# Layer-norm sums in float32r, weight conversions moved earlier, and finer matmul groups in an attention + FFN + gMLP kernel

## The chip, the cores and the metric

One core of a Trainium2 chip runs one program. The metric is the device time in microseconds of one execution, as a median over runs; a profile of one further execution shows where its time goes. TensorE is called PE (its weight loads PEld), VectorE DVE, ScalarE ACT, GpSimd POOL; all DMAs are issued by SyncE (SP).

## What is computed

Four batches of 448 tokens, model width 768, all in float32:

```python
scores = cap * tanh(q @ k.T / 8 / cap)              # 12 heads of 64
x = softmax(scores) @ v                             # heads side by side: (4, 448, 768)
xn = (x - mean(x)) / sqrt(var(x) + 1e-6) * g_ln     # layer norm over the 768 features
x = x + relu(xn @ w_ch1) @ w_ch2                    # FFN, inner width 3072
u, v = split(relu(x @ w_in))                        # gMLP, 512 + 512
v_n = (v - mean(v)) / sqrt(var(v) + 1e-6)
out = (u * (w_spatial @ v_n + b_spatial)) @ w_out
```

## The kernel before

Features lie on partitions: a tile holds 128 features x 448 tokens. A product with float32 accuracy is made of three float32r matmuls: each operand is split into a high part (a copy rounded to float32r) and a low part (value minus high part), and `hi*hi`, `hi*lo`, `lo*hi` are added in PSUM (`mm3`). Attention, and the column sums of the layer norm, use plain float32 matmuls. The program has a lead (attention of batches 0 and 1, with their layer norms), then for each pair of batches the FFN in six groups of 4 hidden blocks (`h_units`, then `y_units`) and the gMLP (`gmlp`: `v_mm`, `u_units`, `sp_units`, `o_units`). Attention of batches 2 and 3 is spread along the first pair's FFN by `drive`.

A weight is loaded as 64-bit halves, converted to float32 on the chip, stored in a DRAM tile `kept_...` for the second pair, and split into its parts (`weight`). The conversion of one block is an ACTIVATE (times `REBASE`), a shift (TENSOR_SCALAR) and two SCALAR_TENSOR_TENSORs on DVE, all into a `wr` buffer; the split is one copy and one subtraction. There are two `w` (raw) and two `wr` buffers. `make` prepares a block ahead of its use, into `rs` buffers; before the change it does so for two blocks of `w1`.

The layer norm of batch b: `x_done` adds the twelve heads' tiles into `acc`; `ln_mean` sums `acc` over partitions on PE with a matrix of ones, then subtracts the mean, multiplies by `g_ln`, splits into parts, squares and adds the squares; `ln_scale` sums the squares on PE, with 4 x 112 tokens as the stationary operand and two columns of ones moving, forms the standard deviation and sends it through DRAM to all partitions, where DVE multiplies the residual `x` by it.

The order of instructions on each engine is made by `Program.plan`, a list scheduler with fixed costs, due times counted in PE's work, and buffer pools: 4 PSUM tiles `bank`, 2 double ones `two`. On the chip each engine then runs its own list in order, so an instruction that waits holds back all those behind it. The trace shows nearly all instructions at one line, L455, the recorder's call (L458 after the change), so they are told apart by tile names.

Of the kernel before, what the change touches and what calls it, by code (L numbers as in the profile page):

```python
# [48 lines left out]

REBASE = 2.0 ** -112  # L50

EARLY = 2
# [410 lines left out]
def attn_ffn_gmlp_kernel(  # L463
# [49 lines left out]
    ones32 = const.tile([128, 2], F32, name="ones32")  # L513
    capt = const.tile([128, 1], F32, name="capt")
# [51 lines left out]
    def weight(kind, j, home=None):  # L566
        if (kind, j) in made:
            return made.pop((kind, j))
        n = width[kind]
        if kind == "ws":  # L570
            t = hs.get()
            SP.dma_start(out=t, in_=source[kind][j])
        elif (kind, j) in kept:
            t = wr.get()[:, 0:n]
            SP.dma_start(out=t, in_=kept[kind, j])
        else:
            raw = w6.get()[:, 0:n]
            SP.dma_start(out=raw.rearrange("p n t -> p (n t)"), in_=source[kind][j].bitcast(I32))
            t = wr.get()[:, 0:n]
            ti = t.bitcast(I32)  # L580
# [9 lines left out]
            SP.dma_start(out=d, in_=t)  # L590
        if home:
# [4 lines left out]
        cp(hi, t, (A, V))  # L596
# [171 lines left out]

    def ln_mean(b):
# [5 lines left out]
        mean, sq = hs.get(), hs.get()  # L775
        A.activation(out=mean, in_=ps, func=ACTF.Copy, scale=1.0 / DM)
# [15 lines left out]
    def ln_scale(b):  # L792
        sq = ln.pop(b).rearrange("p (n c) -> p c n", c=NCT)
        ps = banks.get()
        with prog.group():
            for c in range(NCT):
                T.matmul(out=ps[0:CT, 2 * c:2 * c + 2], lhsT=sq[:, c], rhs=ones32, start=True, stop=True)
        var, rstd = (t[0:CT] for t in tok_t[b % 2])
        V.tensor_scalar(out=var, in0=ps[0:CT, 0:2 * NCT].rearrange("p (c t) -> p c t", t=2)[:, :, 0],
                        scalar1=1.0 / DM, scalar2=1e-6, op0=ALU.mult, op1=ALU.add)  # L800
# [45 lines left out]
    def v_mm(cs):  # L846

        two = [twos.get(), twos.get()]
        os = [banks.get() for _ in range(4)] + [t[:, j] for t in two for j in range(2)]
        os = os[:len(cs)]  # L850
        for k in range(KD):
            hi, lo = weight("wv", k)
            yh, yl = (t.rearrange("p a n -> p (a n)") for t in ysp[k])
            with prog.group():
                for c, o in zip(cs, os):
                    d = slice(c * 128, (c + 1) * 128)
                    for m, (l, r) in enumerate(((yh[:, d], hi), (yh[:, d], lo), (yl[:, d], hi))):
                        T.matmul(out=o, lhsT=l, rhs=r, start=(k == 0 and m == 0), stop=(k == KD - 1 and m == 2))
# [72 lines left out]
    def o_units(b, dt, ws):  # L931

        pss = [banks.get()[:, 0:S] for _ in ws]
        n = len(gs[b])
        with prog.group():
            for k, g in enumerate(gs[b]):
# [8 lines left out]
    def gmlp(bs, nxt):  # L945
# [16 lines left out]
        if nxt:  # L962
            ln_mean(first)
        vn.clear()
        for dts in ([0, 1, 2], *([dt] for dt in range(3, KD))):
            w = [weight("wo", dt) for dt in dts]
            for b in bs:
# [3 lines left out]
                else:  # L971
                    o_units(b, dts[0], w)
        gs.clear()
        if second:
            ln_mean(second)

    def h_units(bs, g, n):
# [3 lines left out]
        for m in steps:  # L981
            w = [weight("w1", j0 + j) for j in range(m)]
            j0 += m
            for b in bs:
                for j in range(m):
                    h_unit(b, w[j])
                    yield 3 * KD

    def y_units(bs, g, last):
# [3 lines left out]
        for b in bs:  # L993
            if b in ln:
                ln_scale(b)
# [42 lines left out]
    def main():  # L1038
# [6 lines left out]
        P.memset(ones32, 1.0)  # L1045
        P.memset(mhalf, -0.5)
# [3 lines left out]
        lead = attend(0, 2 * H, 1.0) + [(H + 2.25, ln_mean, (0,)), (2 * H + 2.25, ln_mean, (1,))]  # L1050
        lead += [(1.0 + j * H / EARLY, make, ("w1", j)) for j in range(EARLY)]
        drive([], lead)
        for p in range(NP):
# [3 lines left out]
                h_units(bs, g, 3 if g == 0 else 2), y_units(bs, g, g == NG - 1))))  # L1057
            n = 2 * H if p + 1 < NP else 0
            drive(units, attend(2 * H * (p + 1), n, 2 * NG * (FG * 3 * KD + KD * 3 * FG) / max(n, 1)))
# [64 lines left out]
```

## Time and profile before

| | |
|---|---|
| median of 3 runs | 1110.94 us (1109.65 to 1113.84) |
| the profiled execution | 1113.14 us, span of its instructions 1111.4 us |
| busy: PE, DVE, ACT | 1094.4, 704.7, 415.6 us |
| mean granted PE clock | 0.995 |
| chain that ended last | PE 92%, DMA 4%, ACT 1%, DVE 1% |
| DMA | 133.88 MB, mean 120 GB/s |

The span runs from the first to the last instruction. Busy time is that in which an engine has an instruction under way; matmuls overlap, so PE's busy time counts their union. The chain is followed back from the last instruction to whatever released each step.

### The profile page before, as it was taken

Reading aid. Unit: us, or ns where it says so; the run is one execution under the profiler, and the core shown is the slowest. Engines: PE = TensorE matmul, PEld = TensorE weight load, DVE = VectorE, ACT = ScalarE, POOL = GpSimd, SP = SyncE. Lnnn points to the kernel's source line nnn. Section 1 sums busy time; section 2 is a strip of 40 time slices with the busy share of each in tenths; the row PEclk is TensorE's granted clock in tenths of the full one; section 3 lists DMA queues with packets and bytes.
Section 4 is the critical chain, followed back from the end, with each engine's and each line's share of the span. In section 5 each row is a group of like instructions: output and inputs, shape, how many; then the busy total and the mean of one; then the engine's idle time right before and its main releaser. Section 6 shows DMA issues by size and latency. Waiting matters only on the chain.

```text
span 1111.4 us, 14151 instructions
## 1 busy us (share of the span) xinstructions
PE 1094.4 (98%) x5380; PEld 899.6 (81%) x5380; DVE 704.7 (63%) x1183; ACT 415.6 (37%) x615; POOL 11.1 (1%) x17
## 2 busy tenths in 40 slices
PE   8989899999999999999999999999999999999998
PEld 2323597987888878978788899999999999998988
DVE  4768789676595776958989964533343433383861
ACT  7978743545334443354444440111111111120412
POOL 0000000000000000000001000000000000000100
PEclk9989999999999999999999999999999999999999
DMA  6545354555654564554475442212121212122303
GB/s 177 126 103 147 121 154 164 173 163 171 171 174 136 158 210 139 165 162 135 152 233 189 157 142 65 67 39 76 38 76 39 67 38 76 45 62 85 102 10 109
DMA packets 80128, 133.88 MB, mean 120 GB/s; under 512 B 35598, under 2 KB 47804, under 8 KB 80060
## 3 DMA queue, kind: packets, MB, share of 16 engines
q1 hardware_dynamic: 80060, 132.98, 40.0%
q8 instruction: 42, 0.69, 0.3%
q14 instruction: 26, 0.21, 0.1%
HBM read 100.91 MB, written 32.03 MB: 120 GB/s over the span
## 4 chain that ended last, share of the span: by engine, by line
PE 92%; DMA 4%; ACT 1%; SPq 1%; DVE 1%; issue 0%; DVEq 0%
PE bank L455 86%; PE two L455 6%; DMA inv<-rc 1%; DMA rc<-sum 1%; DMA hs<-inv 1%; SPq L455 1%; ACT es L455 1%; DMA qk<-in_qk_dram 1%; DMA w<-in_w_dram 1%; ACT hs L455 1%; DMA vt<-in_v_dram 0%; DVE acc L455 0%; DVE x L455 0%; DVE es L455 0%; ACT wr L455 0%
## 5 line engine op out<-in xcount | busy, mean ns | idle before, releaser
L455 PE MATMUL bank<-rs,wh 128*128 128x448 f32 x2232 | 451.5, 362 | 0.0
L455 PEld LDWEIGHTS bank<-rs,wh 128*128 128x128 f32 x2232 | 417.8, 187 | 33.6 <-ACT wr L455 2.8
L455 PE MATMUL bank<-rb,wh 128*128 128x448 f32 x1728 | 350.7, 363 | 0.0
L455 PEld LDWEIGHTS bank<-rb,wh 128*128 128x128 f32 x1728 | 324.8, 188 | 25.1 <-DVE hs L455 3.3
L455 DVE TENSOR_TENSOR x<-bank,x 128x448 f32<-128x448 f32 x144 | 89.5, 623 | 97.5 <-PE bank L455 96.5
L455 ACT ACTIVATE wh<-wr 128x512 fp32r<-128x512 f32 (+1 forms) x89 | 63.2, 710 | 207.4 <-PE bank L455 170.9
L455 ACT ACTIVATE rb<-bank 128x448 fp32r<-128x448 f32 x96 | 52.2, 544 | 222.4 <-PE bank L455 222.3
L455 DVE SCALAR_TENSOR_TENSOR rb<-bank,rb 128x448 fp32r<-128x448 f32 x96 | 59.8, 624 | 112.3 <-ACT rb L455 111.9
L455 DVE TENSOR_TENSOR wh<-wr,wh 128x512 fp32r<-128x512 f32 (+1 forms) x150 | 117.4, 782 | 10.7 <-ACT wh L455 6.0
L455 DVE SCALAR_TENSOR_TENSOR wr<-w,wr 128x512 int32<-128x512 int32 (+1 forms) x152 | 119.2, 785 | 2.2
L455 ACT ACTIVATE wr<-w 128x512 f32<-128x512 f32 (+1 forms) x76 | 57.6, 758 | 84.1 <-DVE wh L455 35.6
L455 ACT ACTIVATE es<-two,qsc 128x896 f32<-128x896 f32 x72 | 70.9, 1009 | 24.7 <-PE two L455 24.4
L455 PE MATMUL two<-qk 64*128 64x448 f32 x288 | 69.6, 584 | 4.2 <-DMA qk<-in_qk_dram 4.2
L455 ACT ACTIVATE es<-es,capt 128x896 f32<-128x896 f32 x72 | 72.2, 1043 | 0.0
L455 DVE CAST wh<-wr 128x512 fp32r<-128x512 f32 (+1 forms) x61 | 28.8, 472 | 66.0 <-PE bank L455 48.6
L455 PE MATMUL bank<-es,vt 128*64 128x448 f32 x288 | 63.8, 557 | 0.5 <-DMA vt<-in_v_dram 0.5
L455 PEld LDWEIGHTS two<-qk 64*128 64x128 f32 x288 | 25.0, 191 | 42.6 <-issue 22.3
L455 DVE TENSOR_TENSOR es<-es,es 128x896 f32<-128x896 f32 x48 | 52.0, 1083 | 3.5 <-ACT es L455 3.2
L455 PEld LDWEIGHTS bank<-es,vt 128*64 128x64 f32 x288 | 18.1, 137 | 41.1 <-issue 30.0
L455 ACT ACTIVATE hs<-bank 128x448 f32<-128x448 f32 x49 | 26.5, 541 | 64.2 <-PE bank L455 63.6
L455 DVE TENSOR_SCALAR wr<-wr 128x512 int32<-128x512 int32 (+1 forms) x76 | 35.8, 471 | 22.8 <-ACT wr L455 22.6
L455 PE MATMUL bank<-wh,rs 128*128 128x512 f32 x144 | 35.6, 395 | 0.0
(79 smaller groups left out, 620.0 us busy)
## 6 DMA issues: line engine op xcount, KB each, us to landing
w<-in_w_dram SPq DMA_DIRECT2D x24, 768.0 KB, 5.3
w<-in_w_dram SPq DMA_DIRECT2D x36, 512.0 KB, 4.1
qk<-in_qk_dram SPq DMA_DIRECT2D x48, 224.0 KB, 3.4
kept_w<-wr SPq DMA_DIRECT2D x24, 384.0 KB, 4.9
kept_w<-wr SPq DMA_DIRECT2D x36, 256.0 KB, 4.2
wr<-kept_w SPq DMA_DIRECT2D x24, 384.0 KB, 3.9
wr<-kept_w SPq DMA_DIRECT2D x36, 256.0 KB, 2.7
out_dram<-hs SPq DMA_DIRECT2D x24, 224.0 KB, 2.1
```

What stands on the lines that cost most here:

```text
L455: fn(*(put(a) for a in args), **{k: put(a) for k, a in kw.items()})
```

## The change

Five things are changed. (1) Both column sums of a layer norm go through `feature_sum`: the summed tile is split into parts on DVE or ACT, and two float32r matmuls with a 128 x 128 matrix of ones sum them. The sum of squares now stands as a row over tokens, so `ln_scale` sends it through DRAM once more to get it as 112 x 4. (2) Centering is a function of its own (`ln_center`), and sums and centering are recorded at other points. (3) Four `w1` blocks instead of two are prepared during the first batch's heads, two of them into `wh` buffers, and the first FFN group takes all four blocks in one step; the conversion's first instruction may run on DVE as well as on ACT. (4) The conversions of the 16 gMLP weight blocks are recorded along the first FFN, from 0.3 to 0.75 of its work; the gMLP then loads the converted blocks. (5) `v_mm` and `o_units` are recorded in smaller groups and take their PSUM tiles in another order.

```diff
+AFTER = 0.3, 0.75, 0
-EARLY = 2
+EARLY = 4
...
+    onesr = const.tile([128, 128], F32R, name="onesr")
...
     def make(kind, j):
         with prog.early():
-            made[kind, j] = weight(kind, j, [rs.get().rearrange("p a n -> p (a n)") for _ in range(2)])
+            made[kind, j] = weight(kind, j, [rs.get().rearrange("p a n -> p (a n)") for _ in range(2)]
+                                   if j < 2 else [t[:, i] for t in (wh.get(),) for i in range(2)])
+    def ahead(kind, j):
+        with prog.early():
+            value(kind, j)
...
-            A.activation(out=t, in_=hi.bitcast(F32), func=ACTF.Copy, scale=REBASE)
+            with prog.either():
+                for e in (A, V) if home is None else (V, A):
+                    if e is A:
+                        A.activation(out=t, in_=hi.bitcast(F32), func=ACTF.Copy, scale=REBASE)
+                    else:
+                        V.tensor_scalar(out=t, in0=hi.bitcast(F32), scalar1=REBASE, scalar2=None, op0=ALU.mult)
...
+    def feature_sum(ps, x):
+        t = rb.get()[:, :, 0:S]
+        cp(t[:, 0], x)
+        sub(t[:, 1], x, f(t[:, 0]))
+        with prog.group():
+            for j in range(2):
+                T.matmul(out=ps, lhsT=onesr, rhs=t[:, j], start=(j == 0), stop=(j == 1))
...
     def ln_mean(b):
         ps = banks.get()[:, 0:S]
-        T.matmul(out=ps, lhsT=ones32[:, 0:1].broadcast_to([128, 128]), rhs=accs[b % 2], start=True, stop=True)
+        feature_sum(ps, accs[b % 2])
...
     def ln_scale(b):
-        sq = ln.pop(b).rearrange("p (n c) -> p c n", c=NCT)
-        ps = banks.get()
-        with prog.group():
-            for c in range(NCT):
-                T.matmul(out=ps[0:CT, 2 * c:2 * c + 2], lhsT=sq[:, c], rhs=ones32, start=True, stop=True)
+        ps = banks.get()[:, 0:S]
+        feature_sum(ps, ln.pop(b))
+        row = hs.get()[0:1]
+        V.tensor_scalar(out=row, in0=ps[0:1], scalar1=1.0 / DM, scalar2=1e-6, op0=ALU.mult, op1=ALU.add)
...
+        d = dram.tile([1, S], F32, name=f"var_{b}")
+        SP.dma_start(out=d, in_=row)
+        SP.dma_start(out=var, in_=d.rearrange("a (n c) -> (a n) c", c=NCT))
...
-        lead = attend(0, 2 * H, 1.0) + [(H + 2.25, ln_mean, (0,)), (2 * H + 2.25, ln_mean, (1,))]
+        lead = attend(0, 2 * H, 1.0) + [(x, fn, (b,)) for x, b in ((H + 3.2, 0), (2 * H + 2.25, 1)) for fn in (ln_mean, ln_center)]
...
-                h_units(bs, g, 3 if g == 0 else 2), y_units(bs, g, g == NG - 1))))
+                h_units(bs, g, FG if g == 0 and p == 0 else 3 if g == 0 else 2), y_units(bs, g, g == NG - 1))))
...
+            if p == 0:
+                later = [("wv", k) for k in range(KD)] + [("wu", i) for i in range(KH)] + [("wo", k) for k in range(KD)]
+                for j, x in enumerate(later):
+                    todo.append((total * (AFTER[0] + (AFTER[1] - AFTER[0]) * j / len(later)), ahead, x))
```

The scheduler's order moves at three places that matter below. First PE, where batch 0's mean is summed, in the middle of the lead (`acc_131` is batch 0's sum of heads, `rb_79` its two parts, `qk` with `two` the scores, `es` and `hs` with `vt` the products with v). Before:

```order
L455 MATMUL bank_147<-qk_115 64x448
L455 MATMUL bank_146<-acc_131,ones_134 128x448
L455 MATMUL bank_148<-es_108,vt_0_118 64x448 x2
L455 MATMUL bank_148<-hs_88,vt_0_118 64x448
L455 MATMUL bank_145<-es_110,ones_133 64x448 x2
L455 MATMUL two_150<-qk_115 128x448 x2
L455 MATMUL two_149<-qk_115 128x448 x2
```

Now:

```order
L458 MATMUL bank_148<-qk_115 64x448
L458 MATMUL two_151<-qk_115 128x448 x2
L458 MATMUL two_150<-qk_115 128x448 x2
L458 MATMUL bank_146<-rb_79,onesr 128x448 x2
L458 MATMUL bank_149<-es_109,vt_0_118 64x448 x2
L458 MATMUL bank_149<-hs_88,vt_0_118 64x448
L458 MATMUL bank_147<-es_110,ones_133 64x448 x2
```

Two groups of score matmuls that stood behind the mean's sum now stand ahead of it.

Next ACT, at the end of the lead, where the third and fourth `w1` blocks were converted before (`wr_102<-w_100` and `wr_103<-w_101` are the conversions' first steps, `rb` an h block's high part, `hs_92` the denominators of batch 1's fifth pair of heads). Before:

```order
L455 ACTIVATE wr_102<-w_100 128x768
L455 ACTIVATE es_112<-es_112,capt 128x896
L455 ACTIVATE rb_79<-bank_146 128x448
L455 ACTIVATE wr_103<-w_101 128x768
L455 ACTIVATE hs_92<-bank_148 128x448
L455 ACTIVATE es_113<-two_149,qsc 128x896
L455 ACTIVATE wh_104<-wr_102 128x768
L455 ACTIVATE x_5_130<-bank_147 128x448
```

Now:

```order
L458 ACTIVATE acc_132<-x_0_125 128x448
L458 ACTIVATE es_111<-es_111,capt 128x896
L458 ACTIVATE rb_81<-bank_148 128x448
L458 ACTIVATE hs_92<-bank_146 128x448
L458 ACTIVATE x_4_129<-bank_147 128x448
L458 ACTIVATE es_113<-two_150,qsc 128x896
L458 ACTIVATE wr_102<-w_100 128x512
```

The two conversions and the copy into `wh_104` no longer stand between the evictions; the next raw weight (width 512) comes after them.

Last DVE, at the start of the lead (`wr_102`, `wr_103` are weights under conversion, `rs_63` and `rs_64` the first one's parts, `es` sums over score blocks for a pair of heads). Before, the first nine instructions on weights and sums:

```order
L455 TENSOR_SCALAR wr_102<-wr_102 128x768
L455 SCALAR_TENSOR_TENSOR wr_102<-w_100,wr_102 128x768 x2
L455 CAST rs_63<-wr_102 128x768
L455 TENSOR_TENSOR rs_64<-wr_102,rs_63 128x768
L455 TENSOR_TENSOR es_110<-es_107,es_108 128x896
L455 TENSOR_TENSOR es_110<-es_110,es_109 128x896
L455 TENSOR_TENSOR es_110<-es_110,hs_87 64x448
L455 TENSOR_TENSOR es_110<-es_110,hs_88 64x448
```

Now:

```order
L458 TENSOR_SCALAR wr_102<-w_100 128x768
L458 TENSOR_SCALAR wr_102<-wr_102 128x768
L458 SCALAR_TENSOR_TENSOR wr_102<-w_100,wr_102 128x768 x2
L458 CAST rs_63<-wr_102 128x768
L458 TENSOR_SCALAR wr_103<-w_101 128x768
L458 TENSOR_TENSOR rs_64<-wr_102,rs_63 128x768
L458 TENSOR_TENSOR es_110<-es_107,es_108 128x896
L458 TENSOR_SCALAR wr_103<-wr_103 128x768
L458 TENSOR_TENSOR es_110<-es_110,es_109 128x896
L458 SCALAR_TENSOR_TENSOR wr_103<-w_101,wr_103 128x768
L458 TENSOR_TENSOR es_110<-es_110,hs_87 64x448
L458 TENSOR_TENSOR es_110<-es_110,hs_88 64x448
```

Conversions of the following weights now stand between the sums of the first pairs of heads, and their first step is on DVE.

## Rows read from the trace of the kernel before

**Rows 1.** The page's first part: busy us (share of the span) and instructions.
```profile
PE 1094.4 (98%) x5380; PEld 899.6 (81%) x5380; DVE 704.7 (63%) x1183; ACT 415.6 (37%) x615; POOL 11.1 (1%) x17
```
**Rows 2.** Windows: stretch, length, busy by engine (instructions), PE clock, DMA share, GB/s.
```profile
138.00:1108.00 970.00, 969.95 (x4816) 849.24 (x4816) 606.07 (x1025) 304.94 (x470) 8.92 (x7) 1.00 0.39 118
...
260.00:450.00 190.00, 190.00 (x961) 153.32 (x958) 128.13 (x201) 82.69 (x116) 0.00 (x0) 1.00 0.56 165
```
**Rows 3.** PE's groups by form: count, busy, mean ns of one, idle before.
```profile
L455 PE MATMUL bank<-rs,wh 128*128 128x448 f32 x2232 | 451.5, 362 | 0.0
...
L455 PE MATMUL bank<-ones,hs 128*112 128x2 f32 x32 | 6.6, 331 | 0.0
...
L455 PE MATMUL bank<-acc,ones 128*128 128x448 f32 x8 | 4.7, 672 | 5.4 <-DVE acc L455 5.4
```
**Rows 4.** PE's instructions in order of time, 683 us on and before (start, us).
```profile
680.54 3.26 PE L455 MATMUL bank<-ones,hs 128*112 128x2 f32 x16
683.67 8.65 PE L455 MATMUL bank<-rb,wh 128*128 128x448 f32 x34
```
**Rows 5.** Windows of two stretches in which the clock fell.
```profile
73.40:80.30 6.90, 5.62 (x14) 1.75 (x14) 5.13 (x9) 3.75 (x7) 0.00 (x0) 0.51 0.34 82
...
680.50:688.00 7.50, 7.50 (x32) 7.06 (x31) 1.66 (x6) 0.54 (x1) 2.02 (x2) 0.77 0.14 35
```
**Rows 6.** PE's instructions in order of time, 70 to 82 us.
```profile
69.58 0.98 PE L455 MATMUL bank<-qk 64*64 64x448 f32 x8
74.68 1.83 PE L455 MATMUL bank<-acc,ones 128*128 128x448 f32 x2 [4.12 <-DVE acc L455]
...
80.74 1.77 PE L455 MATMUL two<-qk 64*128 64x448 f32 x8
```
**Rows 7.** DVE's groups by form: count, busy, mean ns of one, idle before.
```profile
L455 DVE SCALAR_TENSOR_TENSOR wr<-w,wr 128x512 int32<-128x512 int32 x96 | 65.9, 688 | 1.5
...
L455 DVE SCALAR_TENSOR_TENSOR wr<-w,wr 128x768 int32<-128x768 int32 x56 | 53.3, 951 | 0.7
L455 DVE TENSOR_TENSOR es<-es,es 128x896 f32<-128x896 f32 x48 | 52.0, 1083 | 3.5 <-ACT es L455 3.2
...
L455 DVE TENSOR_TENSOR es<-es,hs 64x448 f32<-64x448 f32 x48 | 28.7, 616 | 2.3 <-ACT hs L455 1.7
...
L455 DVE TENSOR_SCALAR wr<-wr 128x512 int32<-128x512 int32 x48 | 20.3, 422 | 13.1 <-ACT wr L455 13.1
...
L455 DVE TENSOR_SCALAR wr<-wr 128x768 int32<-128x768 int32 x28 | 15.5, 555 | 9.7 <-ACT wr L455 9.5
...
L455 DVE CAST rs<-hs 128x448 fp32r<-128x448 f32 x5 | 1.9, 389 | 0.8 <-PE bank L455 0.8
```
**Rows 8.** PE's instructions in order of time, 84 to 142 us.
```profile
100.99 3.90 PE L455 MATMUL bank<-rs,rs 128*128 128x448 f32 x18 [1.57 <-ACT hs L455]
...
113.05 0.97 PE L455 MATMUL bank<-es,ones 128*64 128x448 f32 x4 [0.89 <-ACT hs L455]
...
116.75 3.98 PE L455 MATMUL bank<-rs,rs 128*128 128x448 f32 x18 [0.87 <-ACT x L455]
...
129.04 1.02 PE L455 MATMUL bank<-acc,ones 128*128 128x448 f32 x2 [1.26 <-DVE acc L455]
```
**Rows 9.** ACT's instructions in order of time, 84 to 146 us.
```profile
111.67 0.90 ACT L455 ACTIVATE wr<-w 128x768 f32<-128x768 f32 x1 [3.77 <-DMA w<-in_w_dram]
...
115.43 0.84 ACT L455 ACTIVATE wh<-wr 128x768 fp32r<-128x768 f32 x1 [1.53 <-DVE wr L455]
```
**Rows 10.** ACT's first conversion, and two neighbours on DVE, in order of time.
```profile
8.52 0.89 ACT L455 ACTIVATE wr<-w 128x768 f32<-128x768 f32 x1 [0.50 <-DMA w<-in_w_dram]
...
43.50 1.08 DVE L455 TENSOR_TENSOR es<-es,es 128x896 f32<-128x896 f32 x1
44.50 0.62 DVE L455 COPY hs<-bank 128x448 f32<-128x448 f32 x1
```
**Rows 11.** PE's instructions in order of time: the fourth pair's denominators.
```profile
40.78 0.92 PE L455 MATMUL bank<-es,ones 128*64 128x448 f32 x4
```
**Rows 12.** DVE's instructions in order of time: residual times standard deviation, batch 0.
```profile
152.16 0.63 DVE L455 TENSOR_TENSOR x<-x,hs 128x448 f32<-128x448 f32 x1 [1.84 <-DMA hs<-std]
```

More of the change, by code (lines that the diff above doesn't have):

```diff
@@ L563, in make, with value @@
         with prog.early():
-            made[kind, j] = weight(kind, j, [rs.get().rearrange("p a n -> p (a n)") for _ in range(2)])
-    def weight(kind, j, home=None):
-        if (kind, j) in made:
-            return made.pop((kind, j))
+            made[kind, j] = weight(kind, j, [rs.get().rearrange("p a n -> p (a n)") for _ in range(2)]
[3 more added lines that the diff above has]
+            value(kind, j)
+    def value(kind, j, home=None):
         n = width[kind]
@@ L590, in weight @@
             SP.dma_start(out=d, in_=t)
+        return t
+    def weight(kind, j, home=None):
+        if (kind, j) in made:
+            return made.pop((kind, j))
+        n = width[kind]
+        t = value(kind, j, home)
         if home:
@@ L767, in ln_load, with ln_center @@
             SP.dma_start(out=xts[b % 2][k], in_=xsp[b, k])
+    def feature_sum(ps, x):
[5 more added lines that the diff above has]
+                T.matmul(out=ps, lhsT=onesr, rhs=t[:, j], start=(j == 0), stop=(j == 1))
+    means = {}
     def ln_mean(b):
         ps = banks.get()[:, 0:S]
-        T.matmul(out=ps, lhsT=ones32[:, 0:1].broadcast_to([128, 128]), rhs=accs[b % 2], start=True, stop=True)
-        mean, sq = hs.get(), hs.get()
-        A.activation(out=mean, in_=ps, func=ACTF.Copy, scale=1.0 / DM)
+        feature_sum(ps, accs[b % 2])
+        means[b] = hs.get()
+        A.activation(out=means[b], in_=ps, func=ACTF.Copy, scale=1.0 / DM)
+    def ln_center(b):
+        mean, sq = means.pop(b), hs.get()
         xn[b] = []
@@ L848, in v_mm @@
         two = [twos.get(), twos.get()]
-        os = [banks.get() for _ in range(4)] + [t[:, j] for t in two for j in range(2)]
-        os = os[:len(cs)]
+        os = [t[:, j] for t in two for j in range(2)] + [banks.get() for _ in range(len(cs) - 4)]
         for k in range(KD):
@@ L853, in v_mm @@
             yh, yl = (t.rearrange("p a n -> p (a n)") for t in ysp[k])
[L854 to L858, printed above, removed]
+            for c, o in zip(cs, os):
+                if k in (0, KD - 1) or c == 0:
+                    part = ExitStack()
+                    part.enter_context(prog.group())
+                d = slice(c * 128, (c + 1) * 128)
+                for m, (l, r) in enumerate(((yh[:, d], hi), (yh[:, d], lo), (yl[:, d], hi))):
+                    T.matmul(out=o, lhsT=l, rhs=r, start=(k == 0 and m == 0), stop=(k == KD - 1 and m == 2))
+                if k in (0, KD - 1) or c == cs[-1]:
+                    part.close()
         vs = [es.get().rearrange("p a n -> p (a n)")[:, 0:DH] if i < COUNTS[7] else o for i, o in enumerate(os)]
@@ L931, in o_units @@
     def o_units(b, dt, ws):
-        pss = [banks.get()[:, 0:S] for _ in ws]
+        pss = [banks.get()[:, 0:S]]
+        if len(ws) == 3:
+            two = twos.get()
+            pss += [two[:, j, 0:S] for j in range(2)]
         n = len(gs[b])
-        with prog.group():
-            for k, g in enumerate(gs[b]):
+        for k, g in enumerate(gs[b]):
+            with prog.group():
                 for (hi, lo), ps in zip(ws, pss):
@@ L961, in gmlp @@
         us.clear()
-        if nxt:
-            ln_mean(first)
         vn.clear()
@@ L972, in gmlp @@
                     o_units(b, dts[0], w)
+            if nxt and len(dts) > 1:
+                ln_mean(first)
+                ln_center(first)
+            elif second and dts[0] == KD - 2:
+                ln_mean(second)
         gs.clear()
         if second:
-            ln_mean(second)
+            ln_center(second)
     def h_units(bs, g, n):
@@ L986, in h_units @@
                     h_unit(b, w[j])
+                    if b in ln and j == 1:
+                        ln_scale(b)
                     yield 3 * KD
@@ L1045, in main @@
         P.memset(ones32, 1.0)
+        V.tensor_copy(onesr, ones32[:, 0:1].broadcast_to([128, 128]))
         P.memset(mhalf, -0.5)
@@ L1056, in main @@
             units = chain(*(x for g in range(NG) for x in (
-                h_units(bs, g, 3 if g == 0 else 2), y_units(bs, g, g == NG - 1))))
+                h_units(bs, g, FG if g == 0 and p == 0 else 3 if g == 0 else 2), y_units(bs, g, g == NG - 1))))
             n = 2 * H if p + 1 < NP else 0
-            drive(units, attend(2 * H * (p + 1), n, 2 * NG * (FG * 3 * KD + KD * 3 * FG) / max(n, 1)))
+            total = NG * 2 * (FG * 3 * KD + KD * 3 * FG)
+            todo = []
+            if p == 0:
+                later = [("wv", k) for k in range(KD)] + [("wu", i) for i in range(KH)] + [("wo", k) for k in range(KD)]
+                later = later[AFTER[2]:]
+                for j, x in enumerate(later):
+                    todo.append((total * (AFTER[0] + (AFTER[1] - AFTER[0]) * j / len(later)), ahead, x))
+            drive(units, todo + attend(2 * H * (p + 1), n, 2 * NG * (FG * 3 * KD + KD * 3 * FG) / max(n, 1)))
             gmlp(bs, [b for b in (2 * p + 2, 2 * p + 3) if n])
```

7 lines of the change are left out of this document (1 added, 6 removed).

## Prediction

> **What bounds the kernel now.** I read the page's first part, then the windows, then PE's instructions in order of time. PE is busy for 98% of the span [rows 1], and from 138 us to the end without a gap: 969.95 of 970 us [rows 2]. There a product's matmul takes 451.5 / 2232 = 0.202 us [rows 3]. So after 138 us the time can fall only if PE is given less to do or if its clock falls less, and a faster DVE, ACT or DMA is worth nothing there. In the 138 us before, PE waits, and its waits in order of time show for whom. The reader is to see three kinds of loss: the float32 sums of the layer norms, two stretches at half clock, and waits of the lead.
>
> **The change part by part.**
>
> *Sums in float32r.* Before, the means take 4.7 us of PE and the sums of squares 6.6 us, together 11.3 [rows 3]. Now there are 8 sums of two float32r matmuls with 448 columns, the shape priced above: 16 x 0.202 = 3.2. PE never idles after 138 us, and in the lead it reaches each sum in its own order, so all of the difference is on the path: **8.1 us**. Each sum needs a cast (0.39) and a subtraction (0.62, as other operations on two tensors) first [rows 7], 1.0 us more before it can start. In the FFN and gMLP the new order puts other matmuls ahead of the sums, such as four h blocks (18 matmuls each, 3.6 us) before the first sum of squares of the second pair, so I cost the delay at nothing there; if that cover were gone at all 8 sums, it would take 8 us back.
>
> *The clock after the sums of squares.* The two sums of squares of batches 2 and 3 are 16 matmul records of only 2 columns in 3.26 us; the next 34 matmuls take 8.65 us [rows 4] instead of 34 x 0.202 = 6.9 plus 0.2 for the last one's longer end. The window around them shows a granted clock of 0.77 [rows 5], so part of it is at 1.2 instead of 2.4 GHz. PE did not idle ahead of that, it only did little per instruction. With 448 columns moving this goes: **1.6 us** (bounds 0 and 1.6).
>
> *The wait for batch 0's mean.* PE stands at the sum from about 70.6 to 74.7 us, 4.12 us idle, while DVE waits for the last heads' denominators [rows 6]. Two groups of score matmuls are now ahead of the sum; eight records of that kind take 1.77 us [rows 6]. The cast and subtraction put the sum 1.0 us later. That leaves 4.12 - 1.77 + 1.0 = 3.35: **0.8 us**. The clock is at half afterwards: 0.51 over 5.62 busy us [rows 5], which costs about 2.8, of which 0.9 is the sum itself and already counted. An idle time of 1.57 at 101 us [rows 8] brought no such fall, one of 4.12 did, and 3.35 is nearer the latter. So I let the clock fall again: 0 (bounds 0 and 1.9).
>
> *The third and fourth `w1` block.* Before, they are converted at 105 to 131 us. ACT stands 3.77 us at a conversion whose raw weight has not landed, and later 1.53 us at the copy [rows 9]; behind them in ACT's list are the evictions that free PSUM and the denominators of batch 1's fifth pair. PE then waits 0.89 and 0.87 for ACT's evictions, and 1.26 for batch 1's `acc`, which needs those denominators [rows 8]. With both blocks prepared, ACT evicts at once and PE has 36 more matmuls of batch 0 to do, 7.3 us, before it comes to batch 1's mean. So these three waits go: 0.89 + 0.87 + 1.26 = **3.0 us** (bounds 0 and 3.0). The 1.57 at 101 us hangs on a denominator's transfer and stays; at most it goes too.
>
> *What this costs at the start.* The conversions come to the first 45 us, where PE and ACT are both nearly always busy, and DVE has to keep up with PE. From the first raw weight's landing at 8.52 [rows 10] DVE now has, up to the sums that the fourth pair's denominators need: 12 operations at 0.951 (eight SCALAR_TENSOR_TENSORs, four subtractions of that size), 6 at 0.555 (shifts, casts), 8 at 1.083, 12 at about 0.616 (half-tile sums, copies), some 31 us [rows 7], and four multiplications by `REBASE`, which no DVE row of before shows. Their input is strided. The nearest rows are 0.555 (one contiguous input) and 0.951 (two, one of them this strided one), so 2.2 to 3.8 us. Neighbours overlap: 1.08 us is listed for an instruction whose follower starts 1.00 later [rows 10], over some 40 instructions 3.3 us. DVE is done at 8.5 + 31 + (2.2 to 3.8) - 3.3 = 38.4 to 40.0, or 43.3 without the overlap, against 40.78 when PE wants it [rows 11]. DVE can also stand at the second raw weight, which is now converted while the first is. I take **-0.5 us** (bounds 0 and -2.5). The Trainium skill, VectorE: DVE Perf Modes, section What auto-detection actually checks, lets an operation with a single source in SBUF run at two elements per cycle and asks nothing of the stride; by that the multiplications cost 0.555 each, this term is 0 and the sum 0.5 better. By the row with the strided input DVE is a little too slow for comfort. No run here shows the operation yet.
>
> *The gMLP's weights.* Sixteen blocks, 12 of width 512 and 4 of width 768, at 0.42 + 2 x 0.69 and 0.555 + 2 x 0.951 [rows 7], are 31 us more for DVE, 40 if all their multiplications go there too, in roughly 260 to 450 us. DVE is busy for 128 of 190 us there [rows 2]; 159 to 168 still fit. They leave the first gMLP, where PE is full anyway, so the gain is nothing. The cost is nothing as long as the idle 62 us take them (bounds 0 and -3). The stores are the same in number, and 16 loads are added.
>
> *The variance's second trip through DRAM.* Before, DVE already waits 1.84 us for the broadcast standard deviation [rows 12], with two DMAs in the chain; now there are four. Behind that wait are additions that free PSUM tiles. Four tiles and y blocks of 12 matmuls (2.4 us each) give PE about 7 us of work, so: 0 (bounds 0 and -3).
>
> *Smaller groups in `v_mm` and `o_units`.* Same matmuls, and PE is full there before: 0.
>
> The sum is 8.1 + 1.6 + 0.8 + 3.0 - 0.5 = 13.0 us. The span of 1111.4 becomes 1098.4. The profiled execution took 1113.14, which is 2.2 more than the median of 1110.94; I take the sum off the median: **1098 us**.
>
> **The rivals.** A measurement of this kernel can tell about 0.5% (5.6 us) from no change.
>
> (a) *DVE falls behind at the start.* For it speaks that it has next to no idle time up to 43 us now, and that PE's list holds the score matmuls behind the denominators. Against it, that the sum above ends just in time. The price is 2.5 plus a late second weight, some 4 us in all: 1102.
>
> (b) *The waits at the lead's end only move.* Batch 1's `acc` still hangs on a chain of four DMAs from its fifth pair. If the 3.0 does not come and the two-trip variance costs 1 to 2, the time is 1102 to 1103. Against it speaks that ACT's 3.77 us of standing is what began that delay.
>
> (c) *The change doesn't do what it says.* PE meets each sum before DVE has split the tile. At 1.0 each, 8 us of the 13 are gone, perhaps with another fall of the clock: 1106 to 1108, no change by measurement. Against it speaks the new order around the sums in the FFN; for it, that costs in the scheduler's list are its own.
>
> (d) *Slower.* The place is 260 to 450 us: conversions stand ahead of the sums of score blocks in DVE's list, and PE, in order, stops at each denominator. Attention has about one pair of heads per 34 us there (12 pairs in 406 us), so 5 to 6 pairs. It decides against the change from 13.0 + 5.6 = 18.6 us on, that is from 3.3 us per pair, more than three of the largest conversion steps in a row; the time is then above 1116. DVE's 128 of 190 us speaks against it.
>
> **How the numbers follow.** The forecast, 1094 to 1100 us, has 0.60; (a) 0.13, (b) 0.12, (c) 0.10, (d) 0.05. The best corner adds 1.9 of clock, 1.57 of the wait that stays and 0.5 of DVE to the sum: 1094. The range for 8 in 10 runs from 1093 to 1106 and leaves out (d), most of (c) and little at the low end. Faster by over 0.5% means below 1105.4: the forecast, (a) and (b), 0.85. Within 0.5%: (c), 0.10. Slower: (d), 0.05.
>
> **What would show it.** In the profile after: PE's group with `onesr`, 16 matmuls at about 0.2 us of pace; no fall of the clock near 680 us; an idle time of 3 to 3.5 us at the first of these sums and a half clock behind it; none of the three waits at 113, 117 and 129 us; the start of the gapless stretch at about 131 instead of 138 us. Waits of PE for DVE's `es` sums below 45 us would show (a), at 260 to 450 us (d), and waits for `rb` right before `onesr` (c). I would be wrong if PE has new gaps after the lead, or if DVE's multiplication by `REBASE` takes over 1 us.

## The result and the profile after

The changed kernel takes 1103.18 us (median of 5, 1100.92 to 1104.03) against 1110.97 beside it (5 runs): ratio 0.9919, 95% interval 0.9897 to 0.9941, so 0.6 to 1.0% faster. A later group of runs gave 1102.74 against 1111.14, ratio 0.993 (0.9912 to 0.9947). Some 8.1 us are gained (7.8 and 8.4) where the sum had 13.0. The profiled execution took 1100.92 us, the fastest of its five, with a span of 1099.2; that of before was at its slow end, so the two profiles differ by 12.2 us, more than the medians do.

The page's first part now, beside [rows 1]:

```profile
PE 1086.7 (99%) x5356; PEld 894.1 (81%) x5356; DVE 725.2 (66%) x1235; ACT 390.8 (36%) x580; POOL 12.1 (1%) x17
```

PE is busy for 7.7 us less and idles less. The sums, by form (beside [rows 3]):

```profile
L458 PE MATMUL bank<-rs,wh 128*128 128x448 f32 x2184 | 443.2, 362 | 0.0
...
L458 PE MATMUL bank<-rb,onesr 128*128 128x448 f32 x16 | 5.4, 412 | 2.7 <-DVE rb L458 2.7
```

PE in order of time through the end of the lead, and at the first pair of heads along the FFN (beside [rows 6] and [rows 8]):

```profile
72.07 1.77 PE L458 MATMUL two<-qk 64*128 64x448 f32 x8
76.51 1.40 PE L458 MATMUL bank<-rb,onesr 128*128 128x448 f32 x2 [2.67 <-DVE rb L458]
...
98.68 3.91 PE L458 MATMUL bank<-rs,rs 128*128 128x448 f32 x18 [0.27 <-DVE hs L458]
...
113.58 3.92 PE L458 MATMUL bank<-rs,rs 128*128 128x448 f32 x18 [1.11 <-DVE x L458]
117.34 0.57 PE L458 MATMUL bank<-rb,onesr 128*128 128x448 f32 x2
117.75 7.36 PE L458 MATMUL bank<-rs,wh 128*128 128x448 f32 x36
124.95 0.57 PE L458 MATMUL bank<-rb,onesr 128*128 128x448 f32 x2
...
183.96 0.96 PE L458 MATMUL bank<-es,ones 128*32 128x448 f32 x8
```

The reader is to see: the wait at batch 0's mean is 2.67 us instead of 4.12; of the four waits of [rows 8], 4.59 us together, the first (1.57) is down to 0.27, the third (0.87, at the second group rs,rs) is now 1.11 and for DVE instead of ACT, and the other two are gone; and from 113.6 us on there is no gap (I expected that from about 131). The last row is a marker: PE comes to it at 183.96, and came to it at 191.43 before. So 7.5 of the 12.2 us come from the lead and the first blocks behind it, 4.7 from the rest. For those 4.7 there are 3.0 us of cheaper sums (worked out below) and a fall of the clock near 680 us that cost at most 0.23 x 7.5 = 1.7 [rows 5].

Windows of the same profile (beside [rows 5] and [rows 2]; the column of two decimals after POOL's is the granted clock):

```profile
74.00:84.00 10.00, 7.49 (x28) 2.69 (x30) 9.05 (x16) 6.05 (x11) 0.00 (x0) 0.83 0.37 92
...
675.00:700.00 25.00, 25.00 (x126) 23.44 (x126) 15.35 (x26) 3.59 (x5) 0.00 (x0) 1.00 0.31 80
...
136.00:1090.00 954.00, 954.00 (x4750) 835.25 (x4750) 616.42 (x1056) 278.05 (x427) 9.34 (x7) 1.00 0.40 124
```

Behind batch 0's mean the clock still falls, for less time: 0.83 over 10 us loses at most 1.7 us, 0.51 over 6.9 us lost at most 3.4; both are upper bounds, since PE idles for a part of either window. Near 680 us it stays at 2.4 GHz. Over all runs whose clock is known, span times (1 - mean granted clock), a bound of the same kind, is on average 4.3 us for before (63 runs, clock 0.9961) and 2.1 us for the changed kernel (11 runs, 0.9981).

DVE at the start (beside [rows 7] and [rows 10]):

```profile
8.26 0.56 DVE L458 TENSOR_SCALAR wr<-w 128x768 f32<-128x768 f32 x1 [2.57 <-DMA w<-in_w_dram]
...
12.74 0.56 DVE L458 TENSOR_SCALAR wr<-w 128x768 f32<-128x768 f32 x1 [0.74 <-DMA w<-in_w_dram]
```

The multiplication with a strided input takes 0.56 us. That is what the Trainium skill has (VectorE: DVE Perf Modes, What auto-detection actually checks): two elements per cycle for one source in SBUF, with nothing asked of the stride. PE has no recorded idle time at the lead's first sums of score blocks.

### The profile page after: what moved, and what is told of

Read it like the earlier page. It is cut to its first block, busy times and chain, and to the rows that moved or that the text cites. A ratio compares the mean times of both kernels' runs of the same rounds, so it can differ in the third digit from the quotient of the medians.

```text
span 1099.2 us, 14146 instructions
## 1 busy us (share of the span) xinstructions
PE 1086.7 (99%) x5356; PEld 894.1 (81%) x5356; DVE 725.2 (66%) x1235; ACT 390.8 (36%) x580; POOL 12.1 (1%) x17
## 4 chain that ended last, share of the span: by engine, by line
PE 92%; DMA 3%; DVE 1%; SPq 1%; ACT 1%; issue 0%; DVEq 0%; ACTq 0%
PE bank L458 85%; PE two L458 7%; DMA hs<-inv 1%; DMA inv<-rc 1%; SPq L458 1%; ACT es L458 1%; DMA w<-in_w_dram 1%; DVE es L458 1%; DVE x L458 0%; DMA rc<-sum 0%; ACT hs L458 0%; DVE wr L458 0%; DMA sum<-hs 0%; DVE acc L458 0%; DVE rs L458 0%
## 5 line engine op out<-in xcount | busy, mean ns | idle before, releaser
L458 PE MATMUL bank<-rs,wh 128*128 128x448 f32 x2184 | 443.2, 362 | 0.0
L458 PEld LDWEIGHTS bank<-rs,wh 128*128 128x128 f32 x2184 | 409.0, 187 | 31.2 <-issue 2.1
L458 ACT ACTIVATE wh<-wr 128x512 fp32r<-128x512 f32 (+1 forms) x81 | 58.4, 721 | 198.3 <-PE bank L458 168.6
L458 DVE TENSOR_TENSOR wh<-wr,wh 128x512 fp32r<-128x512 f32 (+1 forms) x150 | 117.3, 783 | 12.2 <-ACT wh L458 8.0
L458 ACT ACTIVATE wr<-w 128x512 f32<-128x512 f32 (+1 forms) x47 | 35.4, 752 | 105.8 <-DMA w<-in_w_dram 62.1
L458 DVE CAST wh<-wr 128x512 fp32r<-128x512 f32 (+1 forms) x69 | 32.0, 464 | 58.2 <-PE bank L458 56.6
L458 ACT ACTIVATE hs<-bank 128x448 f32<-128x448 f32 x44 | 23.7, 541 | 58.0 <-PE bank L458 57.6
L458 DVE TENSOR_TENSOR x<-x,hs 128x448 f32<-128x448 f32 x36 | 21.5, 618 | 24.6 <-DMA hs<-inv 16.2
```

Source lines behind the costliest of these rows:

```text
L458: fn(*(put(a) for a in args), **{k: put(a) for k, a in kw.items()})
```

## The experiments

My theory was that the parts add up as summed: cheaper sums, a quieter clock, a shorter lead, and nothing for the rest. The main rival was that the lead alone, or the order, makes the gain. Each group of runs had the kernel before beside it on its chip; the differences are to that. The changed kernel ran in the last group only; a variant of another group is compared with it by these differences, with 8.1 us for the changed kernel. The ratio is taken over all runs and need not equal that of the medians. The scheduler orders each variant anew, so that undoing a part also moves its neighbours. No run tests by itself where centering is recorded, or that a conversion's first step may run on DVE.

| kernel | median us | before beside | difference | ratio (95%) |
|---|---|---|---|---|
| sums only | 1105.23 | 1110.49 | -5.3 | 0.996 (0.9947 to 0.9973) |
| all sums float32 | 1114.01 | 1110.49 | +3.5 | 1.0025 (1.0014 to 1.0036) |
| two early blocks | 1109.24 | 1110.49 | -1.3 | 0.9994 (0.998 to 1.0009) |
| no conversions ahead | 1100.48 | 1110.49 | -10.0 | 0.9909 (0.9896 to 0.9921) |
| means float32 | 1109.01 | 1112.59 | -3.6 | 0.9969 (0.9957 to 0.9981) |
| squares float32 | 1111.57 | 1112.59 | -1.0 | 0.9987 (0.9972 to 1.0002) |
| later mean | 1107.15 | 1112.59 | -5.4 | 0.9951 (0.9938 to 0.9963) |
| old groups | 1107.49 | 1112.59 | -5.1 | 0.9954 (0.9942 to 0.9967) |
| the changed kernel again | 1102.74 | 1111.14 | -8.4 | 0.993 (0.9912 to 0.9947) |
| no conversions ahead, again | 1100.96 | 1111.14 | -10.2 | 0.9911 (0.9896 to 0.9926) |
| the same, old groups | 1106.07 | 1111.14 | -5.1 | 0.9953 (0.994 to 0.9966) |
| the same, two early blocks | 1108.45 | 1111.14 | -2.7 | 0.9977 (0.9967 to 0.9988) |

**Sums only**: the kernel before with `feature_sum` in both places, and the sums of squares inside `h_units` as after.

```diff
-        T.matmul(out=ps, lhsT=ones32[:, 0:1].broadcast_to([128, 128]), rhs=accs[b % 2], start=True, stop=True)
+        feature_sum(ps, accs[b % 2])
...
+                    if b in ln and j == 1:
+                        ln_scale(b)
```

> The kernel before with the float32r sums alone (and with the place of the sums of squares inside the first FFN group that they need). My theory: the sums themselves are worth about 5.5 us (11.3 us of PE busy time before, 5.4 after), the fall of the clock near 680 us 1.6, and the order around batch 0's mean 1: 7 to 8 us faster than before, about 1103.5, no half clock near 680 us, and the three waits at 113, 117 and 129 us still there. Rival one, the conversions make the gain: within 3 us of before. Rival two, DVE's split of the summed tiles stands in PE's way at each sum: under 4 us faster, with PE idle right ahead of the onesr matmuls.

It brought 5.3 us, less than I expected and more than the 4 of my second rival. Its profile has a new gap in the gMLP, between the two halves of batch 2's mean:

```profile
616.70 0.36 PE L455 MATMUL bank<-rb,onesr 128*128 128x448 f32 x1
618.30 0.47 PE L455 MATMUL bank<-rb,onesr 128*128 128x448 f32 x1 [1.24 <-DVE rb L455]
```

That is my rival (c): PE meets the sum before DVE has subtracted the high part. In the lead, from 90 to 133 us, PE now stops for ACT and DVE nine times, for 0.25 to 0.80 us.

**All sums in float32**: the changed kernel with the two float32 forms of before in `ln_mean` and `ln_scale`. The scheduler keeps the new order in the main, but puts batch 0's mean ahead of the two groups of score matmuls again, as it was before.

```diff
-        feature_sum(ps, accs[b % 2])
+        T.matmul(out=ps, lhsT=ones32[:, 0:1].broadcast_to([128, 128]), rhs=accs[b % 2], start=True, stop=True)
...
-        feature_sum(ps, ln.pop(b))
...
+                T.matmul(out=ps[0:CT, 2 * c:2 * c + 2], lhsT=sq[:, c], rhs=ones32, start=True, stop=True)
```

> The changed kernel with the float32 sums of before put back, all else as changed. My theory: it loses the 7 us that the sums are worth and keeps about 3 from the early w1 blocks: 1107 to 1109, with the half clock back behind the sums of squares of batches 2 and 3. Rival, the gain is the conversions': within 2 us of the changed kernel.

It is slower than before, 11.6 us above the changed kernel. PE and then the clock in its profile:

```profile
121.07 1.81 PE L458 MATMUL bank<-ones,hs 128*112 128x2 f32 x8 [1.24 <-DVE hs L458]
122.74 5.44 PE L458 MATMUL bank<-rs,wh 128*128 128x448 f32 x18
...
192.02 0.96 PE L458 MATMUL bank<-es,ones 128*32 128x448 f32 x8
```
```profile
74.00:84.00 10.00, 6.78 (x20) 2.38 (x22) 6.44 (x11) 4.05 (x8) 0.00 (x0) 0.66 0.31 82
...
118.00:128.00 10.00, 8.77 (x36) 7.79 (x35) 8.83 (x15) 4.60 (x7) 1.28 (x1) 0.83 0.34 100
655.00:676.00 21.00, 21.00 (x107) 19.91 (x106) 15.36 (x31) 7.76 (x15) 2.65 (x2) 1.00 0.24 57
```

From the marker to the end it takes 1110.2 - 192.0 = 918.2 us, the changed kernel 1099.2 - 184.0 = 915.2. PE has no gap there in either, and four of the eight sums lie there: 3.0 us for four, so about 6.0 for eight, if the four in the lead save as much (an estimate), is what float32r saves in PE's own time, not 8.1. The other 5 us of its profile are in the lead: a clock of 0.83 behind the wait and the two-column sum at 121 us (at most 1.7 us), 0.66 instead of 0.83 behind batch 0's mean (at most another 1.7, in a place where the clock differs between executions of one kernel, see the last section), longer waits, and a start that was 1.1 us later; these overlap in part with the sums' own time, since batch 0's mean runs at half clock in both.

**Means in float32** and **squares in float32**: the same, for one of the two sums each.

> The changed kernel with the four means taken in float32 as before; the sums of squares stay in float32r. My theory (each float32 sum costs its own matmul time, and only the two-column sums of squares let the clock fall): four means at 1.18 us (4.7 by rows 3) instead of four at about 0.55, so +2.5 us, and batch 0's mean waits for nothing that is split, -1 us and the half clock as before: 1104 to 1106. Rival (the 11 us that all sums in float32 cost are the wait at batch 0's mean): 1108 or more.

> The changed kernel with the four sums of squares as before, in float32 with two moving columns, and without the variance's trip through DRAM; the means stay in float32r. My theory: 6.6 us for the sums (rows 3) instead of 2.2, so +4.4, and a fall of the clock to half behind such a sum, in the lead or in the gMLP, another +1.7 or more: 1107 to 1110, and a stretch of granted clock under 1 behind a group ones,hs. Rival (the clock falls by the idle time ahead of a sum alone): +4.4, 1105 to 1107, and no new stretch at half clock.

Against the changed kernel's 8.1 us the float32 means lose 4.5 and the float32 squares 7.1; together 11.6, as much as both at once, but that is partly chance: in the profiles of these two PE also stands 4.06 and 1.42 us between 320 and 540 us, at waits that the changed kernel's profile lacks (see "No conversions ahead"). For the means my figure was too low. PE stands 4.34 us at batch 0's mean instead of 2.67, since the sum stands two groups of score matmuls earlier in PE's list. The rival's bound of 1108 was reached, on a chip where the kernel before was 1.6 us slower; its reason fails, since the squares alone lose 7.1 with a wait of 2.69 there. The profile of the means, of 1113.21 us, is the slowest of its twelve runs.

For the squares the loss was about what I expected, 7.1 against 6.1 or more, though 1111.57 lies above my 1107 to 1110. A float32 sum of squares takes 1.46 us to the next instruction's start (657.28 to 658.74), a float32r one 0.41 (117.34 to 117.75 above): 4.2 for four. My mechanism for the rest was wrong: no new fall of the clock lies behind the two-column sums, the profile has the 1.42 along the FFN and a start later by 2.2 us (batch 1's first sums at 59.84 instead of 57.64), neither of them at a sum of squares. PE, and the window around the sums near 657 us:

```profile
657.28 1.60 PE L458 MATMUL bank<-ones,hs 128*112 128x2 f32 x8
658.74 11.05 PE L458 MATMUL bank<-rs,wh 128*128 128x448 f32 x54
```
```profile
655.00:676.00 21.00, 21.00 (x108) 19.90 (x107) 15.13 (x31) 8.39 (x16) 2.65 (x2) 1.00 0.12 37
```

Before, two such sums stood back to back for 3.26 us [rows 4]; the new order puts 54 matmuls between them, and the clock stays up with either form. That speaks for the new place of `ln_scale`, at least as much as for float32r, as what ends the fall near 680 us; with one profile of each it is not shown, since a fall can come or stay away between executions of one kernel.

**Two early blocks**, once in the changed kernel and once without the conversions ahead:

```diff
-EARLY = 4
+EARLY = 2
...
-                h_units(bs, g, FG if g == 0 and p == 0 else 3 if g == 0 else 2), y_units(bs, g, g == NG - 1))))
+                h_units(bs, g, 3 if g == 0 else 2), y_units(bs, g, g == NG - 1))))
```

> The changed kernel with two w1 blocks prepared ahead instead of four, and the first FFN group in steps of three and one again. My theory: the waits of PE for ACT's evictions and for batch 1's mean come back, 3 us slower than the changed kernel, about 1105 to 1106, with ACT standing at a raw weight between 100 and 130 us. Rival, the waits only moved: within 1 us of the changed kernel.

> The kernel without the gMLP's conversions along the first FFN, and with two w1 blocks prepared and a first group of three and one, as before. My theory (the third and fourth w1 block are worth the 3.0 us that I summed, and a little more where PE stands at the next two sums): 3 to 5 us more than with four, with waits of PE for ACT or DVE between 85 and 135 us. Rival (two prepared blocks are as good, and the 6 us of the earlier run came from its late v at the start and the conversions in the FFN): within 1.5 us of the kernel with four.

6.8 and 7.5 us worse than with four, more than twice the 3.0 that I summed. (The first keeps the conversions along the FFN, and its profile has 1.28 us of waits between 320 and 540 us.) ACT in the second of them:

```profile
111.10 0.90 ACT L458 ACTIVATE wr<-w 128x768 f32<-128x768 f32 x1 [3.53 <-DMA w<-in_w_dram]
111.90 0.99 ACT L458 ACTIVATE es<-two,qsc 128x896 f32<-128x896 f32 x1
...
116.96 0.85 ACT L458 ACTIVATE wh<-wr 128x768 fp32r<-128x768 f32 x1 [3.63 <-DVE wr L458]
117.71 0.99 ACT L458 ACTIVATE es<-two,qsc 128x896 f32<-128x896 f32 x1
```

It is the standing of [rows 9] again: a raw weight that has not landed, then a copy that waits for DVE, each with an eviction behind it. PE's waits follow at once, and the clock:

```profile
112.95 1.02 PE L458 MATMUL two<-qk 64*128 64x448 f32 x4 [1.28 <-ACT es L458]
...
120.70 1.02 PE L458 MATMUL two<-qk 64*128 64x448 f32 x4 [0.92 <-ACT es L458]
```
```profile
74.00:84.00 10.00, 8.62 (x26) 2.90 (x26) 9.80 (x18) 5.96 (x10) 0.00 (x0) 0.66 0.34 93
...
115.00:130.00 15.00, 13.36 (x54) 9.20 (x56) 13.64 (x20) 11.44 (x17) 1.45 (x1) 0.89 0.31 93
```

The clock of 0.89 over 15 us behind the short waits near 113 and 121 us costs at most 1.7 us; that comes on top of the waits, and my term had only these. The 0.66 behind batch 0's mean is no mark of this variant: with four blocks and no conversions ahead, the same sum was followed by 1.00 in one execution and by 0.66 in another.

The second variant can also be set beside "sums only". It has the sums in float32r too, the smaller groups and the new order, and neither the two further blocks nor the conversions ahead; it gains 2.7 us where the sums alone gain 5.3. So the rest of the change probably costs some 2.6 us as long as two blocks are prepared (the two ran on different chips, and their intervals just overlap), and a part of the 7 is what the four blocks make good. Which part of the change costs it, no run separates.

**No conversions ahead**, twice:

```diff
-                later = later[AFTER[2]:]
+                later = []
```

> The changed kernel without the conversions of the gMLP's weights along the first FFN; they are converted in the first gMLP as before. My theory: PE has no gap there in either kernel, so the time stays within 1 us of the changed kernel. Rival one, these conversions carry a good part of the gain: 4 us or more slower. Rival two, they cost: 2 us or more faster.

> The changed kernel without the gMLP's conversions along the first FFN, a second time. My theory: no wait of PE over 0.5 us from 140 us to the end, and 1 to 3 us less than the changed kernel on this chip, ratio about 0.990. Rival (the conversions ahead cost nothing and bring nothing): within 1 us of the changed kernel.

> The changed kernel itself, beside three variants on one chip. Five of the variants that convert the gMLP's weights along the first FFN showed PE standing 0.6 to 3 us in all between 320 and 400 us, where ACT stood 2 to 3.4 us at a raw weight that had not landed; the changed kernel's own profile and the variant without these conversions showed none. My theory (these conversions cost 0 to 3 us, by the run): a ratio of 0.990 to 0.995, and 1 to 3 us more than the variant without. Rival (the waits belong to those variants alone): no wait over 0.5 us from 140 us on, and the same time as the variant without.

It beats both kernels: 10.0 and 10.2 us below before, about 2 below the changed kernel. On one chip its runs lie from 1100.84 to 1101.80, the changed kernel's from 1100.17 to 1105.63; the ratios' intervals overlap, so the 2 us are likely rather than settled. The changed kernel's own two profiles, of executions of 1100.92 and 1100.17 us, show no wait behind it; five variants with these conversions do, for 1.28 us (two early blocks), 1.29 (old groups), 1.42 (float32 squares), 2.73 (later mean) and 4.06 (float32 means) between 320 and 540 us, and "all sums in float32" does not; of the four variants without them none does. The differences of those five therefore hold a share that is not their own part's. Old groups show one form of the wait, on ACT and then on PE; the float32 means have it on PE as well:

```profile
362.97 0.66 ACT L458 ACTIVATE wr<-w 128x512 f32<-128x512 f32 x1 [3.12 <-DMA w<-in_w_out_dram]
363.54 1.89 ACT L458 ACTIVATE es<-two,qsc 128x896 f32<-128x896 f32 x2
```
```profile
364.58 1.02 PE L458 MATMUL two<-qk 64*128 64x448 f32 x4 [1.29 <-ACT es L458]
```
```profile
371.88 1.02 PE L458 MATMUL two<-qk 64*128 64x448 f32 x4 [1.41 <-ACT es L458]
```

It is my rival (d) in little, and on another engine: not DVE has too much to do, but ACT stands at a raw weight, and the scores' eviction waits behind it. That this is also what the changed kernel's slower runs lose is likely and not shown, as no profile fell on one of them. Without the conversions ahead PE has no gap in that stretch:

```profile
136.00:540.00 404.00, 404.00 (x2035) 331.94 (x2034) 309.30 (x506) 156.79 (x217) 1.04 (x1) 1.00 0.53 161
```

**Old groups**, in the changed kernel and without the conversions ahead (the cut shows the o products; the v products likewise, and both get their PSUM tiles in the old order again, so that grouping and tiles are undone together):

```diff
-        for k, g in enumerate(gs[b]):
-            with prog.group():
+        with prog.group():
+            for k, g in enumerate(gs[b]):
```

> The changed kernel with the groups of the gMLP's v and o products as before. My theory: 0, since PE has no gap there either way: 1102 to 1104, with the gapless stretch as it was. Rival (smaller groups let PE go on where a wide group would wait for a bank): slower by 1 us or more, with waits of PE between 540 and 720 us.

> The kernel without the gMLP's conversions along the first FFN, and with the groups of the v and o products as before. Where these conversions stood, wide groups had PE wait 1.6 us behind the v products at 568 us, for an eviction, and 2.1 us between the two halves of a mean's sum at 618 us, for DVE. My theory (the wide groups do it, since a group of 48 or 54 matmuls takes its banks at once and leaves nothing to put beside a sum): the same two waits and 3 to 4 us more than the kernel without the conversions. Rival (the weights' early conversion does it): neither wait, and the same time.

3.0 and 5.1 us worse, where I had costed the groups at nothing. The first had both waits that its rival named, 1.61 us at 570 us for ACT and 2.12 at 620 us for DVE. PE, DVE and the clock of the second:

```profile
614.97 0.36 PE L458 MATMUL bank<-rb,onesr 128*128 128x448 f32 x1
617.66 0.47 PE L458 MATMUL bank<-rb,onesr 128*128 128x448 f32 x1 [2.33 <-DVE rb L458]
617.97 7.35 PE L458 MATMUL bank<-rs,wh 128*128 128x448 f32 x28
```
```profile
613.18 1.15 DVE L458 TENSOR_TENSOR rs<-qk,rs 128x448 fp32r<-128x448 f32 x2
614.25 0.68 DVE L458 SCALAR_TENSOR_TENSOR wr<-w,wr 128x512 int32<-128x512 int32 x1
614.86 1.15 DVE L458 TENSOR_TENSOR qk<-bank,vt 128x448 f32<-128x448 f32 x2
615.92 1.15 DVE L458 TENSOR_TENSOR qk<-qk,hs 128x448 f32<-128x448 f32 x2
616.99 0.61 DVE L458 TENSOR_TENSOR rb<-acc,rb 128x448 fp32r<-128x448 f32 x1
```
```profile
612.00:630.00 18.00, 15.68 (x72) 13.71 (x71) 15.80 (x30) 10.70 (x20) 0.00 (x0) 0.91 0.44 156
```

DVE is busy without a break, and the subtraction for the sum has its turn at 617 us; PE is there at 615, ahead of the o products. In the changed kernel the same sum stands at 628.14, behind 72 of the o products' matmuls. The wait of 2.33 is followed by a clock of 0.91 over 18 us, at most 1.6 us more: 3.9 of the 5.1. The other wait that I expected, behind the v products, did not come here; with the conversions ahead it did.

**Later mean**:

```diff
-        lead = attend(0, 2 * H, 1.0) + [(x, fn, (b,)) for x, b in ((H + 3.2, 0), (2 * H + 2.25, 1)) for fn in (ln_mean, ln_center)]
+        lead = attend(0, 2 * H, 1.0) + [(x, fn, (b,)) for x, b in ((H + 4.4, 0), (2 * H + 2.25, 1)) for fn in (ln_mean, ln_center)]
```

> The changed kernel with batch 0's mean put later in the lead's list (4.4 instead of 3.2 units behind the heads): five groups of products that do not hang on the denominators stand ahead of the sum now, 2.6 us at full clock. If the 2.67 us of waiting at 73.8 us is on the path to the end: it is gone, and with it the stretch at half clock behind it, together up to 4 us less: 1098 to 1101. Rival (batch 0's chain from its mean to its first FFN block, 22 us, only starts later, and PE waits at that block instead): no change, 1102 to 1104, with a wait of 2 to 3 us ahead of the first group rs,rs.

Neither held; it is 2.7 us worse. PE, then DVE:

```profile
79.74 0.47 PE L458 MATMUL bank<-rb,onesr 128*128 128x448 f32 x1 [1.74 <-ACT rb L458]
81.20 0.47 PE L458 MATMUL bank<-rb,onesr 128*128 128x448 f32 x1 [0.99 <-DVE rb L458]
```
```profile
75.29 0.20 DVE L458 RECIPROCAL rc<-rc 128x7 f32<-128x7 f32 x1 [1.67 <-DMA rc<-sum]
77.79 0.62 DVE L458 TENSOR_TENSOR x<-x,hs 128x448 f32<-128x448 f32 x1 [2.30 <-DMA hs<-inv]
78.45 0.63 DVE L458 TENSOR_TENSOR acc<-acc,x 128x448 f32<-128x448 f32 x1
```

The sum moved on PE, but DVE's list moved with it: DVE now stands at the next pair's denominators (RECIPROCAL) ahead of the last addition to `acc`. The wait is as long, later, and in two parts, and batch 1's sum waits another 2.02 us at 124 us. The 2.7 are not all its own: the profile, of the slowest of five runs, has the 2.73 us of waits along the FFN as well.

## Why the prediction was right, and where its terms were off

The range held the time and the sign was right, but the median lies above my likeliest case (1094 to 1100), at a time that I had given to rivals (a) and (b), 1102 to 1103, and neither came as I described it. That the range held is in part luck. Term by term:

- **Sums in float32r, 8.1**: about 6.0, from the four sums behind the marker. The failed step is "together 11.3": I took the listed busy time of the float32 sums for their price. It holds batch 0's mean at half clock (1.83 us of the 4.7), and the ends of matmuls that overlap the next ones.
- **Clock, 1.6**: over the runs at most 2.2 us less are lost, at both places together. The place was right (none near 680 us now), the reason at most half: in one profile the clock fell behind two such sums back to back, in two it stayed up behind sums apart.
- **Batch 0's mean, 0.8**: 4.12 became 2.67 in one profile and 2.70 in another, some 1.4. I had left 3.35: the sum's first matmul needs only the cast, not the subtraction (they start on DVE at 76.06 and 76.49 us, the sum at 76.51). That the clock falls again was right for the first; in the second, after the same idle time, it did not, and the window of that execution reads

```profile
74.00:84.00 10.00, 7.11 (x36) 2.53 (x35) 8.68 (x16) 6.09 (x11) 0.00 (x0) 1.00 0.37 97
```

- **Third and fourth `w1` block, 3.0**: the waits of [rows 8] went from 4.59 to 1.38 us, 3.2 less, which is my size by chance. Of the three that I priced, 1.11 of 3.02 is left, so they gave 1.9; another 1.3 came from the 1.57 at 101 us, which I let stand because it "hangs on a denominator's transfer", and which fell to 0.27. To take the blocks away again costs 7, in which the clock falls as well.
- **DVE at the start, -0.5**: in the changed kernel's two profiles DVE was in time, and rival (a) did not come; four variants with the same start show it in little, with 0.28 to 0.93 us of PE's waits for DVE's `es` sums below 45 us. But PE reaches the first heads of batch 1 some 1.5 us later than before in the profile (its sums at 57.64 instead of 56.13). Of that 1.3 us lie in one group of score matmuls, on PE before and now and in its weight loads now:

```profile
52.73 1.91 PE L455 MATMUL bank<-qk 64*64 64x448 f32 x8
...
52.86 3.19 PE L458 MATMUL bank<-qk 64*64 64x448 f32 x8
...
54.30 0.19 PEld L458 LDWEIGHTS bank<-qk 64*64 64x64 f32 x2 [0.83 <-DMA qk<-in_qk_dram]
55.09 0.19 PEld L458 LDWEIGHTS bank<-qk 64*64 64x64 f32 x2 [0.60 <-DMA qk<-in_qk_dram]
```

The group waits for transfers of q and k, which the modelled ends of PE's matmuls hide (before, one of its weight loads waited 0.75; in the second profile of the changed kernel PE itself shows 0.25 of idle time for them). The prediction had no term for transfers at the start. Why they land later is open.
- **gMLP weights, 0 (bounds 0 and -3)**: about -2. I asked only whether DVE has room, and not what stands behind the conversion on ACT when its raw weight is late, though [rows 9] showed just that in the lead. The variants show this wait, the changed kernel's own two profiles do not.
- **Variance's second trip, 0**: right; PE has no gap there.
- **Smaller groups, 0**: this step failed. "PE is full there before" was true and beside the point: the sum with its split needs work to stand behind, the groups (or the tile order that goes with them) supply it, and without them rival (c) comes, 1.2 to 2.3 us, with a fall of the clock behind the longest.

6.0 + 2.2 + 1.4 + 3.2 - 1.5 - 2 = 9.3, against 7.8 and 8.4 measured; the rest is within the intervals, and the terms mix single profiles with averages over runs, so this is an estimate. What was too high is the sums' term, by 2.1; what was missing are the 1.0 more at the start and the 2 of the gMLP's weights; three other terms were too low by 0.2 to 0.6.

Undone one by one, the sums cost 11.6, the early blocks 7 and the groups 3 to 5 us, more than 20 together, where the whole change brings 8. The parts do not add up: most of what undoing one costs is a wait, and a clock that falls behind it, that the others had covered.

## What to carry to other kernels

A part costed at nothing because the engine is full there has to be asked what it covers once the other parts are in. Where an engine runs its list in order, a conversion put ahead costs what stands behind it when its transfer is late, even where that engine is idle for most of the time (ACT here is busy for 36% of the span). And putting a waiting instruction later does not remove its wait if the chain that it waits for is ordered by the same move.

## What the hardware showed that I had not expected

The four two-column float32 matmuls of a sum of squares, which the trace shows as eight records, take 1.46 us to the next instruction's start (657.28 to 658.74), 0.18 a record, hardly less than the 0.202 of a float32r matmul with 448 columns: here two columns instead of 448 save next to nothing.

The same idle time, 2.67 and 2.70 us ahead of the same sum, was followed by a granted clock of 0.83 over 10 us in one execution and 1.00 in another; without the conversions ahead it was 0.66 after 2.82 us and 1.00 after 3.10. The Trainium skill (TensorE: Matmul & The Clock Gate, Part 1: The HAM clock gate) says that the monitor's window is free-running and does not start with the kernel, so that the point of a change varies; these executions fit that, and no run here shows the cause. A fall of the clock is to be costed over runs: this kernel's mean granted clock was between 0.996 and 1.000 in eleven.
